# A fused scan and gated MLP: the opening's gate products by token tile, moments and copies handed between engines

## The chip, the core and the metric

The kernel runs on one core of one Trainium2 chip. Times are device microseconds of one execution. The kernel before took 182.35 us, the median of three runs (182.21 to 182.36). One further execution was profiled; its times are used for the working. The engines go by the profile's names: PE is TensorE's matmul, PEld its weight load, DVE is VectorE, ACT is ScalarE, POOL is GpSimd, and SP issues the DMAs (SPq is its queue).

## What is computed

There are 2048 tokens of width 448. A layer norm is followed by two branches that meet at the end:

```python
xn = layernorm(x)                                  # x: [1, 2048, 448]
# A: a diagonal complex recurrence over the tokens
Lam_bar = exp(exp(log_dt) * (Lambda_re + 1j * Lambda_im))
Bu = xn @ (((Lam_bar - 1) / Lam)[:, None] * B).T
h[t] = Lam_bar * h[t - 1] + Bu[t]
s = 2 * real(h @ C.T) + xn * Dskip
# B: a gated MLP, 448 -> 1792 -> 448
hF = sigmoid(xn @ w_gate) * (xn @ w_up)
out = x + s * silu(hF @ w_down)
```

Inputs and output are bfloat16.

## The kernel before

**Tiling.** The tokens go in four chunks of 512, each of four token tiles of 128. The MLP's 1792 features go in 14 feature tiles (`ft`) of 128. A product for one feature tile and one chunk has the features on the partitions and 512 tokens in one PSUM bank. The depth 448 is cut for the gate into three pieces of 128 rows and a tail of 64, and for the up product likewise with other pieces, so that the two tails (`wt`, rows 0 to 63 for the gate and 64 to 127 for up) run beside each other in the two halves of the array.

**Order.** Every engine runs its instructions in the order in which the program writes them (`keep_order`). A planner (`fill`, `rest`, `at`) lays VectorE's pieces of the recurrence between groups, and after the opening TensorE runs pairs of units (`group`, products of 64 rows at L514), the first of which is (4, 5), then (6, 7), (-1, 8), (-2, 9) and so on; negative numbers are the recurrence's input products `bu`. Eight PSUM banks are handed out in turn.

**The opening** is what lies ahead of group (4, 5). It is written out by hand, from L929 to L1015:

- SP's queue issues the token tiles of chunk 0, the weights' columns 0 to 511 (`load_w(sync, 0, 512)`, L150), columns 512 to 1279 with the tails first (L158), chunk 1's tokens, then, further down, four transposing loads of B (`emit_b`, L294), and columns 1280 to 1791 (L1025). ScalarE's queue issues the three vectors log_dt, Lambda_im and Lambda_re into `rows` (L142).
- TensorE runs products of no use (`warm`, L200) in stretches of 26, 5, 2 and 6, and between them turns the three vectors (`turn_twice`, L205 to L207, into `tp_v`) and the first two normed token tiles (`ln_turn`, L286, four transposes into `tp_x`).
- The layer norm of tiles 0, 1 and 3 takes its moments by VectorE (`ln_stats`, L216 and L217), its root by ScalarE as a Ln and an Exp (`ln_inv`, L249 and L250). Tile 2's moments are sums by ScalarE (L224, L227, L231) and its root is a power by POOL (L244). VectorE writes the normed tile (`ln_norm`, L272) and copies the turned tile out of PSUM (`ln_out`, L289) for all four tiles.
- ScalarE copies the turned vectors (`emit_vecs`, L316), makes dt (L321), from which POOL makes the angles (`emit_angles`, L326 to L328). ScalarE then makes the whole turns of four rows (`emit_whole`, L424), VectorE the fractions and their magnitudes (`emit_frac` L429, `emit_abs` L435), and ScalarE sines and cosines (L440, L443), after a table load that a dummy Silu brings (L962).
- Feature tiles 0 to 2 hold six banks. When tiles 0 and 1 are turned, the gate products of their 256 tokens run (L713), then the up products; the turns of tiles 2 and 3 lie between them. Then the tails' halves (L706) for 256 and 256 tokens, then feature tile 3, then the remaining products of tokens 256 to 511.
- ScalarE takes tanh of the gate (L719), VectorE halves the up product into `ub` (`up_copy`, L1000), and VectorE's product of the two (L723) gives `hF`. These free the banks for groups (4, 5) and (6, 7).

Of the kernel before, what the change touches and what calls it, by code (L numbers as in the profile page):

```python
# [14 lines left out]
ACT = mybir.ActivationFunctionType  # L15

S_TOK = 2048
D = 448
F = 1792
P = 128  # L20
TC = 512
HC = TC // 2
# [10 lines left out]
GATE_K, UP_K = (0, 2, 3), (0, 1, 3)  # L33
# [3 lines left out]
MAGIC = 12582912.0  # L37
CLAMP = 1.0 - 2e-6
LN_AND_EXP = 6
SIN_SCALE = TWO_PI * CLAMP  # L40


# [29 lines left out]
def kernel(  # L72
# [17 lines left out]
    nc = tc.nc  # L90
    pe, act, dve, pool, sync = nc.tensor, nc.scalar, nc.vector, nc.gpsimd, nc.sync
# [32 lines left out]
    def load_w(eng, f0, f1, tails_first=False):  # L124
        def rows(mat, r0, r1):
            m = mat[r0:r1, f0:f1]
            return m.rearrange("(kt p) f -> p kt f", p=P) if r1 - r0 > P else m

        eng.dma_start(out=wg[:, 1:3, f0:f1], in_=rows(B_w_gate, 192, 448))
        eng.dma_start(out=wg[:, 0, f0:f1], in_=rows(B_w_gate, 0, 128))  # L130
        up = ((wu[:, 0:2, f0:f1], rows(B_w_up, 0, 256)), (wu[:, 2, f0:f1], rows(B_w_up, 320, 448)))
        tails = ((wt[0:64, f0:f1], rows(B_w_gate, 128, 192)), (wt[64:128, f0:f1], rows(B_w_up, 256, 320)))
        for o, i in (tails + up if tails_first else up + tails):
            eng.dma_start(out=o, in_=i)
# [20 lines left out]
            x_t.append(w.tile([P, TPC, D], BF16, name="x3", tag="tc_re"))  # L155
        sync.dma_start(out=x_t[c][:], in_=x_src[:, c * TPC:(c + 1) * TPC, :])

    load_w(sync, 512, 1280, True)  # L158
    load_x(1)

    ctr = {}
# [36 lines left out]
    def warm(n, t=ident):  # L198
        for _ in range(n):
            pe.matmul(warm_ps[:], lhsT=t[:, 0:P], rhs=t[:, 0:P], start=True, stop=True)  # L200
# [13 lines left out]
    def ln_stats(t):  # L214
        stats = cp.tile([P, 6], FP32, name="stats")
        dve.bn_stats(out=stats[:], in_=x_t[t // TPC][:, t % TPC, :])  # L216
        dve.bn_aggr(out=mv[:, t, :], in_=stats[:])  # L217
# [4 lines left out]
    def ln_sum(t):  # L222
        c, j = divmod(t, TPC)
        act.activation(junk[:], x_t[c][:, j, :], ACT.Copy, accum_out=sums[:, t, 0:1])  # L224

    def ln_mean(t, n):
        act.activation(mv[:, t:t + n, 0:1], sums[:, t:t + n, 0:1], ACT.Copy, scale=1.0 / D)  # L227

    def ln_square(t):
        c, j = divmod(t, TPC)  # L230
        act.activation(junk[:], x_t[c][:, j, :], ACT.Square, bias=mv[:, t, 0:1], scale=-1.0,  # L231
                       accum_out=sums[:, t, 1:2])
# [15 lines left out]
    def ln_inv(t):  # L248
        act.activation(lnv[:, t, :], mv[:, t, 1:2], ACT.Ln, bias=epsb[:])  # L249
        act.activation(rsd[:, t, :], lnv[:, t, :], ACT.Exp, scale=-0.5)  # L250

    def ln_pow_of(t, n, var, scale):
        pool.tensor_scalar(out=ve[:, t:t + n, :], in0=var, scalar1=scale, scalar2=EPS, op0=ALU.mult, op1=ALU.add)
        ln_pow(t, n)
# [30 lines left out]
        for kt in range(KT):  # L285
            pe.transpose(tps[j % 2][:, kt, :], xb[:, j, K_ROWS[kt]:K_ROWS[kt] + P], ident[:])  # L286

    def ln_out(j):
        dve.tensor_copy(out=xnT[0][:, :, j * P:(j + 1) * P], in_=tps[j % 2][:])  # L289

# [21 lines left out]
    def emit_vecs():  # L314
        vec = w.tile([P, KT, 3], FP32, name="vec")
        act.copy(out=vec[:], in_=tp_v[:, :, 0:3])  # L316
        K.update(vec=vec)

    def emit_dt():
        vec, dt_b = K["vec"], w.tile([P, KT], BF16, name="dt_b")  # L320
        act.activation(dt_b[:], vec[:, :, 0], ACT.Exp)  # L321
        K.update(dt=dt_b, lim=vec[:, :, 1], lre=vec[:, :, 2])

    def emit_angles():
        theta, arg_r, turn, r_col = col("theta"), col("arg_r"), col("turn"), col("r_col")
        pool.tensor_tensor(out=theta[:], in0=K["dt"][:], in1=K["lim"], op=ALU.mult)  # L326
        pool.tensor_single_scalar(out=turn[:], in_=theta[:], scalar=1.0 / TWO_PI, op=ALU.mult)
        pool.tensor_tensor(out=arg_r[:], in0=K["dt"][:], in1=K["lre"], op=ALU.mult)  # L328
        K.update(arg=arg_r)
        K.update(theta=theta, turn=turn, r=r_col)  # L330
# [12 lines left out]
    def emit_anf():  # L343
        dve.tensor_single_scalar(out=K["anf"][:].bitcast(I32), in_=K["nf"][:].bitcast(I32), scalar=0x7FFFFFFF,
                                 op=ALU.bitwise_and)
# [76 lines left out]
    def emit_whole(pt):  # L422
        whole = sp.tile([P, HC], I32, name="whole", tag=("ta", "tb", "tcs", "tb")[pt])
        act.activation(whole[:], iota_f[:], ACT.Copy, scale=K["turn"][:, pt:pt + 1])  # L424
        K[pt] = whole

    def emit_frac(pt):
        f = sp.tile([P, HC], FP32, name="frac", tag="wv")
        dve.scalar_tensor_tensor(out=f[:], in0=iota_f[:], scalar=K["turn"][:, pt:pt + 1], in1=K[pt][:],  # L429
                                 op0=ALU.mult, op1=ALU.subtract)  # L430
        K[pt] = f

    def emit_abs(pt):
        af = sp.tile([P, HC], FP32, name="afrac", tag="td")
        dve.tensor_single_scalar(out=af[:].bitcast(I32), in_=K[pt][:].bitcast(I32), scalar=0x7FFFFFFF,  # L435
                                 op=ALU.bitwise_and)
        K[pt, 1] = af

    def emit_sin(pt):
        act.activation(spm[:, pt, 0, HC:TC], K[pt][:], ACT.Sin, scale=(SIN_SCALE if pt < 3 else sgp[:, 0:1]))  # L440

    def emit_cos(pt):
        act.activation(cosT[:, pt, HC:TC], K[pt, 1][:], ACT.Sin, scale=-TWO_PI, bias=hpi[:])  # L443
# [7 lines left out]
    def emit_neg(pt):  # L451
        dve.tensor_single_scalar(out=spm[:, pt, 1, HC:TC], in_=spm[:, pt, 0, HC:TC], scalar=-1.0, op=ALU.mult)
# [251 lines left out]
    def gu_half(c, ft, i, t, first, n0, n1):  # L704
        p0, kt = ((0, 1), (64, 2))[i]
        pe.matmul(t[:, n0:n1], lhsT=wt[p0:p0 + 64, ft * P:(ft + 1) * P], rhs=xnT[c][p0:p0 + 64, kt, n0:n1],  # L706
                  start=first, stop=not first)

    def gu_wholes(c, ft, gt, ut, first, n0=0, n1=TC, which=(0, 1), ks=(0, 1, 2), last=True):
        f0, f1 = ft * P, (ft + 1) * P  # L710
        for t, wm, kts in [((gt, wg, GATE_K), (ut, wu, UP_K))[i] for i in which]:
            for k in ks:
                pe.matmul(t[:, n0:n1], lhsT=wm[:, k, f0:f1], rhs=xnT[c][:, kts[k], n0:n1],  # L713
                          start=(first and k == 0), stop=(not first and last and k == 2))


    def gu_out(ft, gt, ub):
# [191 lines left out]
    def ln_plan(c):  # L909
# [14 lines left out]
        for j in range(TPC):  # L924
# [3 lines left out]
    dummy = w.tile([P, 1], FP32, name="dummy")  # L928
    act.add_instruction(mybir.InstLoadActFuncSet(name=nc.get_next_instruction_name(), act_func_set_id=LN_AND_EXP,  # L929
                                                 ins=[], outs=[]))  # L930
    warm(26, junk)
    turn_twice(tp_v, rows, 3)
    tps = [ps.tile([P, KT, P], BF16, name="tp_x", tag="bank", bufs=8) for _ in range(2)]
    gus = [(bank("g_ps"), bank("u_ps")) for _ in range(3)]
    warm(5)

    ln_stats(0)
    ln_inv(0)
    emit_vecs()
    ln_stats(1)  # L940
    ln_inv(1)
    emit_dt()
    emit_angles()
    ln_sum(2)
    ln_norm(0, 0)
    ln_turn(0, 0)
    warm(2)
    ln_norm(0, 1)
    ln_turn(0, 1)
    warm(6)  # L950
    ln_out(0)
    ln_out(1)
    ln_mean(2, 1)
    ln_square(2)
    ln_pow_of(2, 1, sums[:, 2:3, 1:2], 1.0 / D)
    ln_stats(3)
    emit_whole(0)
    ln_inv(3)
    for pt in (1, 3, 2):
        emit_whole(pt)  # L960
    act.activation(K["r"][:], K["arg"][:], ACT.Exp)
    act.activation(dummy[:], hpi[:], ACT.Silu)  # L962

    emit_frac(0)
    ln_norm(0, 2)
    ln_norm(0, 3)
    for ft in range(3):
        gu_wholes(0, ft, *gus[ft], True, 0, HC, (0,))
    for ft in range(3):
        gu_wholes(0, ft, *gus[ft], True, 0, HC, (1,), (0, 1))  # L970
    ln_turn(0, 2)
    ln_out(2)
    for ft in range(3):
        gu_wholes(0, ft, *gus[ft], False, 0, HC, (1,), (2,), False)
    ln_turn(0, 3)
    ln_out(3)
    emit_abs(0)
    for pt in (1, 3, 2):
        emit_frac(pt)
        emit_abs(pt)  # L980
    gus.append((bank("g_ps"), bank("u_ps")))
    for n0 in (0, HC):
        for ft in range(3):
            for i in range(2):
                gu_half(0, ft, i, gus[ft][i], n0 > 0, n0, n0 + HC)
    for i in range(2):
        gu_half(0, 3, i, gus[3][i], True, 0, TC)
    for ft in range(4):
        gu_wholes(0, ft, *gus[ft], False, (0 if ft == 3 else HC), TC)
    emit_steps()  # L990
    emit_den()
    for pt in (0, 1, 3):
        emit_sin(pt)
        emit_cos(pt)
        if pt == 0:
            emit_neg(pt)
    ubs = [fp.tile([P, TC], BF16, name="ub") for _ in range(4)]

    def up_copy(ft):
        dve.tensor_single_scalar(out=ubs[ft][:], in_=gus[ft][1][:], scalar=0.5, op=ALU.mult)  # L1000

    for ft in range(4):
        gu_out(ft, gus[ft][0], ubs[ft])
        up_copy(ft)
        if ft == 1:
            emit_neg(1)
            emit_neg(3)
            emit_sin(2)
            emit_cos(2)
            emit_anf()  # L1010
            emit_step_sines()
    emit_neg(2)
    for pt, ft in ((0, 5), (1, 5), (2, 8), (3, 11)):
        at(0, ft, 0.0, lambda pt=pt: emit_mirror(pt))
# [7 lines left out]
    for cc in range(2):  # L1022
        for kt in (0, 2):
            emit_b(cc, kt)
    load_w(sync, 1280, F)  # L1025
    sync.dma_start(out=skip[:], in_=A_Dskip.partition_broadcast(P))
    load_x(2)

# [140 lines left out]
```

## Time and profile before

| | |
|---|---|
| median of three runs | 182.35 us (182.21 to 182.36) |
| the profiled execution | 182.26 us |
| its span | 180.5 us (1.76 us lie around it) |
| PE busy | 176.2 us, 98% of the span |
| DVE busy | 163.4 us, 91% |
| ACT busy | 115.1 us, 64% |
| POOL busy | 23.1 us, 13% |
| first gate product starts | 6.38 us |
| group (4, 5) starts | 13.56 us |

A line of the timeline gives the start and the length in us, the engine, the source line, the operation, what it writes and reads, the shape and how many instructions are merged into the line; in brackets stands the idle time before it and who ended it. Products overlap in the array, so the length of a merged line holds a fixed tail of some 0.2 us after the last start; the starts tell the pace. A line of the waits names who waited, for whom, and then us in total, times and the longest. A DMA line ends with the time from issue to landing.

### The profile page before, as it was taken

What the parts mean: (1) busy time and instruction counts of PE and PEld (TensorE: products, weight loads), DVE (VectorE), ACT (ScalarE), POOL (GpSimd) and SP (SyncE); (2) the same over time, 40 slices, a digit from 0 to 9 for tenths busy, and PEclk for the clock granted to TensorE, in tenths of its full rate; (3) what the DMA queues carried; (4) which work ended last, traced back from release to release, by engine and by line L of the source; (5) the groups of instructions that cost most, each with busy time, mean ns of one, the idle gap of its engine ahead of it and who ended that gap; (6) DMA issues with size and microseconds to landing.
All of it is one profiled execution on the core that took longest, in us unless ns stands there. A gap on an engine that the chain in (4) does not pass through costs nothing.

```text
span 180.5 us, 4326 instructions
## 1 busy us (share of the span) xinstructions
PE 176.2 (98%) x1637; PEld 88.2 (49%) x1637; DVE 163.4 (91%) x332; ACT 115.1 (64%) x240; POOL 23.1 (13%) x54
## 2 busy tenths in 40 slices
PE   7999999999999999999999999999999999999992
PEld 7764444445544444544544444544554444545552
DVE  4889999899999879999999999599999999499993
ACT  4999878979577887988177667047137577144100
POOL 3525668522000000003000000000000000000000
PEclk9999999999999999999999999999999999999999
DMA  5899998983442005021710020030010100011012
GB/s 150 239 292 211 245 176 168 356 185 77 99 83 53 16 4 131 5 69 36 89 31 0 4 56 2 4 102 0 4 29 0 35 0 2 4 53 51 0 32 73
DMA packets 26348, 14.27 MB, mean 79 GB/s; under 512 B 16083, under 2 KB 26070, under 8 KB 26326
## 3 DMA queue, kind: packets, MB, share of 16 engines
q1 hardware_dynamic: 26320, 13.98, 33.7%
q8 instruction: 13, 0.21, 0.5%
q14 instruction: 9, 0.07, 0.2%
q10 hardware_dynamic: 6, 0.00, 0.0%
HBM read 7.69 MB, written 1.84 MB: 53 GB/s over the span
## 4 chain that ended last, share of the span: by engine, by line
PE 97%; DVE 1%; issue 0%; DVEq 0%
PE g_ps L514 25%; PE u_ps L514 19%; PE d_ps L514 18%; PE bu L514 12%; PE y_ps L514 11%; PE d_ps L1112 6%; PE warm_ps L200 2%; PE g_ps L713 2%; PE u_ps L713 1%; PE tp_x L286 1%; DVE sg L860 0%; PE g_ps L706 0%; DVE o_l L866 0%; PE u_ps L706 0%; DVE xnT L289 0%
## 5 line engine op out<-in xcount | busy, mean ns | idle before, releaser
L514 PE MATMUL u_ps<-xnT,wu 64*128 64x512 bf16 x312 | 61.4, 376 | 0.0
L514 PE MATMUL g_ps<-xnT,wg 64*128 64x512 bf16 x312 | 53.4, 376 | 0.0
L752 ACT ACTIVATE sig<-g_ps 128x512 bf16<-128x512 f32 x52 | 29.2, 597 | 28.6 <-PE g_ps L514 28.0
L514 PE MATMUL bu<-xnT,bT 64*128 64x512 bf16 x168 | 37.4, 376 | 0.0
L514 PE MATMUL d_ps<-wd,hF 64*128 64x448 bf16 x336 | 32.3, 349 | 0.0
L514 PEld LDWEIGHTS <-wu 64*128 64x128 bf16 x312 | 22.4, 94 | 18.5
L752 ACT CAST ub<-u_ps 128x512 bf16<-128x512 f32 x52 | 29.3, 606 | 0.9 <-DVE hF L723 0.8
L514 PEld LDWEIGHTS <-wg 64*128 64x128 bf16 x312 | 18.9, 94 | 18.3 <-issue 0.4
L514 PEld LDWEIGHTS <-hF 64*128 64x128 bf16 x336 | 16.4, 94 | 15.6
L611 DVE TENSOR_TENSOR_SCAN wv<-r_col,st,ta 128x512 bf16<-128x512 f32 x18 | 22.7, 1277 | 0.2
L514 PE MATMUL y_ps<-ct,h 64*128 64x448 bf16 (+2 forms) x203 | 22.1, 343 | 0.0
L749 DVE TENSOR_TENSOR hF<-sig,ub 128x512 bf16<-128x512 bf16 x52 | 21.0, 413 | 0.4 <-ACT ub L752 0.3
L514 PEld LDWEIGHTS <-bT 64*128 64x128 bf16 x168 | 15.8, 94 | 10.0
L514 PE MATMUL g_ps<-xnT,wt 64*128 64x512 bf16 x52 | 19.6, 376 | 0.0
L514 PE MATMUL u_ps<-xnT,wt 64*128 64x512 bf16 x52 | 19.6, 376 | 0.0
L514 PEld LDWEIGHTS <-h 64*128 64x128 bf16 (+1 forms) x203 | 11.6, 95 | 9.9
L776 ACT ACTIVATE sigd<-d_ps 128x448 bf16<-128x448 f32 x12 | 6.6, 553 | 15.0 <-PE d_ps L514 15.0
L592 ACT CAST bus<-bu 128x512 bf16<-128x512 f32 x24 | 14.3, 597 | 1.7 <-PE bu L514 1.6
L514 PEld LDWEIGHTS <-wt 64*128 64x128 bf16 x104 | 9.8, 94 | 6.2
L831 DVE TENSOR_TENSOR o_t<-y_ps,xn 128x448 bf16<-128x448 f32 x12 | 6.9, 617 | 4.8 <-PE y_ps L514 4.8
L1112 PE MATMUL d_ps<-wd,hF 128*128 128x448 bf16 x56 | 10.9, 353 | 0.0
L244 POOL TENSOR_TENSOR rsd<-ve,mhalf 128x2 f32<-128x2 f32 (+2 forms) x5 | 4.6, 922 | 44.2 <-PE bu L514 44.1
(153 smaller groups left out, 239.7 us busy)
## 6 DMA issues: line engine op xcount, KB each, us to landing
wd<-in_B_w_down_dram SPq DMA_DIRECT2D x1, 1568.0 KB, 7.3
x<-in_A_x_dram SPq DMA_DIRECT2D x3, 448.0 KB, 5.0
out_dram<-o_t SPq DMA_DIRECT2D x6, 224.0 KB, 2.1
wg<-in_B_w_gate_dram SPq DMA_DIRECT2D x2, 256.0 KB, 3.6
wu<-in_B_w_up_dram SPq DMA_DIRECT2D x2, 256.0 KB, 3.7
bsw<-bus SPq DMA_DIRECT2D x4, 128.0 KB, 2.8
wsw<-wv SPq DMA_DIRECT2D x8, 64.0 KB, 1.9
c_re<-in_A_C_re_dram SPq DMA_DIRECT2D x1, 392.0 KB
```

The costliest lines, as they stand in the source:

```text
L200: pe.matmul(warm_ps[:], lhsT=t[:, 0:P], rhs=t[:, 0:P], start=True, stop=True)
L244: pool.tensor_tensor(out=rsd[:, t:t + n, :], in0=ve[:, t:t + n, :], in1=mhalf[:, 0:n, :], op=ALU.pow)
L286: pe.transpose(tps[j % 2][:, kt, :], xb[:, j, K_ROWS[kt]:K_ROWS[kt] + P], ident[:])
L514: m = pe.matmul(self.t[:, n0:n1], lhsT=lhsT, rhs=rhs, start=self.done == 1, stop=self.done == self.n)
L592: empty = [lambda cc=cc: act.copy(out=bus[:, cc, :], in_=pst[cc][:]) for cc in range(2)]
L611: dve.tensor_tensor_scan(out=T["wv"][:, cc, :], data0=rb, data1=T["ta"][:, cc, :], initial=(0.0 if c == 0 else st[pt][:, cc, :]), op0=mul, ...
L713: pe.matmul(t[:, n0:n1], lhsT=wm[:, k, f0:f1], rhs=xnT[c][:, kts[k], n0:n1], start=(first and k == 0), stop=(not first and last and k == 2))
L749: dve.tensor_tensor(out=h[:], in0=sig[:], in1=ub[:], op=ALU.mult)
L752: u.empty = [lambda: act.activation(sig[:], gt[:], ACT.Sigmoid), lambda: act.copy(out=ub[:], in_=ut[:])]
L776: act.activation(sigd[:], ds[j][:], ACT.Sigmoid)
L831: dve.tensor_tensor(out=two_runs(o[:, i, :], HD, HD), in0=two_runs(ys[c, j + 2 * i][:], HD, HD), in1=xn_runs(c, j + 2 * i), op=ALU.add)
L1112: pe.matmul(ds[j][:], lhsT=hF[c, ft][:, j * P:(j + 1) * P], rhs=wd[:, ft, :], start=ft == 0, stop=ft == FT - 1)
```

## The change

Only the opening and the cut between two weight loads change. What it does, engine by engine:

- **TensorE**: 17 products ahead of the turn of the vectors in place of 26, 14 behind it in place of 5, and 3 in place of 6 after the turn of tile 1. The gate products of feature tiles 0 to 2 run for token tile 0 alone (128 columns) and then for token tile 1, depth piece by depth piece over the three feature tiles. Each bank is opened by one product with `start`; all later ones add with `start=False`, also to columns not yet written. The tails' halves of tokens 256 to 511 run by token tile as well.
- **ScalarE**: the vectors, dt and the angles come ahead of the roots of tiles 0 and 1; whole turns 0 and 1 come ahead of the norms. It copies turned tile 1 out of PSUM. It no longer takes tile 2's moments, and it makes tile 2's root. The table is loaded by an explicit instruction. Tanh of feature tiles 0 and 1 comes after the first sine and cosine, tanh 2 after the third pair, tanh 3 after the last.
- **VectorE**: moments of tiles 2 and 3 one after the other behind the copy of tile 0. Fractions 0 and 1 come behind the copy of tile 3, fractions 3 and 2 behind the first two up copies.
- **POOL**: tile 2's power goes.
- **SP**: the second weight load has columns 512 to 1151 and the last one columns 1152 to 1791.

```diff
-    load_w(sync, 512, 1280, True)
+    load_w(sync, 512, 1152, True)
...
-    def ln_out(j):
-        dve.tensor_copy(out=xnT[0][:, :, j * P:(j + 1) * P], in_=tps[j % 2][:])
+    def ln_out(j, by_act=False):
+        (act.copy if by_act else dve.tensor_copy)(out=xnT[0][:, :, j * P:(j + 1) * P], in_=tps[j % 2][:])
...
-                  start=first, stop=not first)
+                  start=first, stop=False)
...
+    def gu_whole(c, ft, i, t, k, n0, n1, first=False, last=False):
+        pe.matmul(t[:, n0:n1], lhsT=(wg, wu)[i][:, k, ft * P:(ft + 1) * P],
+                  rhs=xnT[c][:, (GATE_K, UP_K)[i][k], n0:n1], start=first, stop=last)
...
-    warm(26, junk)
+    warm(17, junk)
     turn_twice(tp_v, rows, 3)
...
-    warm(5)
-
+    warm(14)
+
+    emit_vecs()
+    emit_dt()
+    emit_angles()
     ln_stats(0)
     ln_inv(0)
-    emit_vecs()
     ln_stats(1)
     ln_inv(1)
-    emit_dt()
-    emit_angles()
-    ln_sum(2)
+    for pt in (0, 1):
+        emit_whole(pt)
     ln_norm(0, 0)
     ln_turn(0, 0)
     warm(2)
     ln_norm(0, 1)
     ln_turn(0, 1)
-    warm(6)
+    warm(3)
     ln_out(0)
-    ln_out(1)
-    ln_mean(2, 1)
-    ln_square(2)
-    ln_pow_of(2, 1, sums[:, 2:3, 1:2], 1.0 / D)
-    ln_stats(3)
-    emit_whole(0)
-    ln_inv(3)
-    for pt in (1, 3, 2):
-        emit_whole(pt)
+    ln_out(1, True)
+    emit_whole(3)
+    for t in (2, 3):
+        ln_stats(t)
+    for t in (2, 3):
+        ln_inv(t)
+    emit_whole(2)
     act.activation(K["r"][:], K["arg"][:], ACT.Exp)
-    act.activation(dummy[:], hpi[:], ACT.Silu)
-
-    emit_frac(0)
+    act.add_instruction(mybir.InstLoadActFuncSet(name=nc.get_next_instruction_name(), act_func_set_id=SILU_AND_SIN,
+                                                 ins=[], outs=[]))
     ln_norm(0, 2)
     ln_norm(0, 3)
-    for ft in range(3):
-        gu_wholes(0, ft, *gus[ft], True, 0, HC, (0,))
-    for ft in range(3):
-        gu_wholes(0, ft, *gus[ft], True, 0, HC, (1,), (0, 1))
+
+    def firsts(i, ks, n0, n1, first=None):
+        for k in ks:
+            for ft in range(3):
+                gu_whole(0, ft, i, gus[ft][i], k, n0, n1, k == first)
+
+    firsts(0, (1, 2, 0), 0, P, 1)
+    firsts(0, (1, 2, 0), P, HC)
+    firsts(1, (0, 1), 0, HC, 0)
     ln_turn(0, 2)
     ln_out(2)
-    for ft in range(3):
-        gu_wholes(0, ft, *gus[ft], False, 0, HC, (1,), (2,), False)
+    firsts(1, (2,), 0, HC)
     ln_turn(0, 3)
     ln_out(3)
-    emit_abs(0)
-    for pt in (1, 3, 2):
+    for pt in (0, 1):
         emit_frac(pt)
         emit_abs(pt)
...
-    for n0 in (0, HC):
+    for n0, n1 in ((0, HC), (HC, HC + P), (HC + P, TC)):
         for ft in range(3):
             for i in range(2):
-                gu_half(0, ft, i, gus[ft][i], n0 > 0, n0, n0 + HC)
+                gu_half(0, ft, i, gus[ft][i], False, n0, n1)
...
+    tables(0)
+    out(0)
+    out(1)
+    emit_neg(0)
+    for pt in (3, 2):
+        emit_frac(pt)
+        emit_abs(pt)
+    tables(1)
+    tables(3)
+    emit_neg(1)
+    out(2)
+    emit_neg(3)
+    tables(2)
+    out(3)
...
-    load_w(sync, 1280, F)
+    load_w(sync, 1152, F)
```

Here `tables(pt)` is the sine and cosine of a row, and `out(ft)` is the tanh and the up copy of a feature tile. Up and whole products of tokens 256 to 511, and of feature tile 3, keep their order.

More of the change, by code (lines that the diff above doesn't have):

```diff
@@ L39 @@
 LN_AND_EXP = 6
+SILU_AND_SIN = 18
 SIN_SCALE = TWO_PI * CLAMP
@@ L706, in gu_half @@
         pe.matmul(t[:, n0:n1], lhsT=wt[p0:p0 + 64, ft * P:(ft + 1) * P], rhs=xnT[c][p0:p0 + 64, kt, n0:n1],
-                  start=first, stop=not first)
[L709 to L714, printed above, removed]
+                  start=first, stop=False)
+    def gu_whole(c, ft, i, t, k, n0, n1, first=False, last=False):
+        pe.matmul(t[:, n0:n1], lhsT=(wg, wu)[i][:, k, ft * P:(ft + 1) * P],
+                  rhs=xnT[c][:, (GATE_K, UP_K)[i][k], n0:n1], start=first, stop=last)
     def gu_out(ft, gt, ub):
@@ L988 @@
     for ft in range(4):
-        gu_wholes(0, ft, *gus[ft], False, (0 if ft == 3 else HC), TC)
+        for i in range(2):
+            for k in range(3):
+                gu_whole(0, ft, i, gus[ft][i], k, (0 if ft == 3 else HC), TC, last=k == 2)
     emit_steps()
     emit_den()
[L992 to L996, printed above, removed]
     ubs = [fp.tile([P, TC], BF16, name="ub") for _ in range(4)]
@@ L1000, in up_copy, with tables, out @@
         dve.tensor_single_scalar(out=ubs[ft][:], in_=gus[ft][1][:], scalar=0.5, op=ALU.mult)
-    for ft in range(4):
+    def tables(pt):
+        emit_sin(pt)
+        emit_cos(pt)
+    def out(ft):
         gu_out(ft, gus[ft][0], ubs[ft])
         up_copy(ft)
[L1005 to L1011, printed above, removed]
+    tables(0)
[12 more added lines that the diff above has]
+    out(3)
+    emit_anf()
+    emit_step_sines()
     emit_neg(2)
```

## The prediction

> **What bounds the kernel now.** I read the chain of work that ended last first, then the waits of TensorE, then TensorE's timeline over the opening. The chain (part 4 of the page) and TensorE's waits up to 40 us, each as engine, line and releaser with total us, times and longest:
>
> ```profile
> PE 97%; DVE 1%; issue 0%; DVEq 0%
> ```
> ```profile
> PE warm_ps L200 <- DVE junk L177: 1.0, 1, 1.0
> PE g_ps L713 <- DVE xnT L289: 0.2, 1, 0.2
> ```
>
> TensorE is the bound, and after the first gate product it waits for no one that this view names. The stream behind the opening is closed, so a change that touches only the opening is worth what it moves the start of the first group of pairs, (4, 5), and nothing else. The timeline of TensorE (start, length, line, operation, count):
>
> ```profile
> 3.86 0.23 PE L205 MATMUL tp_v<-ident,rows 3*128 3x3 bf16 x3
> ...
> 4.19 0.71 PE L200 MATMUL warm_ps<-ident 128*128 128x128 bf16 x5
> 4.70 0.63 PE L286 MATMUL tp_x<-ident,xn 128*128 128x128 bf16 x4
> ...
> 6.38 1.14 PE L713 MATMUL g_ps<-xnT,wg 128*128 128x256 bf16 x9 [0.18 <-DVE xnT L289]
> 7.43 0.83 PE L713 MATMUL u_ps<-xnT,wu 128*128 128x256 bf16 x6
> 8.09 0.39 PE L286 MATMUL tp_x<-ident,xn 128*128 128x128 bf16 x4
> 8.32 0.49 PE L713 MATMUL u_ps<-xnT,wu 128*128 128x256 bf16 x3
> 8.64 0.39 PE L286 MATMUL tp_x<-ident,xn 128*128 128x128 bf16 x4
> 8.96 0.28 PE L706 MATMUL g_ps<-xnT,wt 64*128 64x256 bf16 x1
> 9.15 0.28 PE L706 MATMUL u_ps<-xnT,wt 64*128 64x256 bf16 x1
> ...
> 10.20 0.50 PE L713 MATMUL g_ps<-xnT,wg 128*128 128x256 bf16 x3
> ...
> 13.56 0.82 PE L514 MATMUL g_ps<-xnT,wg 64*128 64x512 bf16 x6
> ```
>
> Starts of equal products stand 0.109 us apart at 256 columns, 0.216 at 512, and 0.055 for a transpose of 128. The work from 6.38 to 13.56 is then 36 products of 256 columns (3.92), six of 512 (1.30), eight transposes (0.44), six half pairs of 256 (0.65) and one of 512 (0.22): 6.53 us of the 7.18. The other 0.65 is what can be won there, and two pieces of it belong to the weights' DMAs:
>
> ```profile
> 7.42 0.33 PEld L713 LDWEIGHTS <-wu 128*128 128x128 bf16 x4 [0.18 <-DMA wu<-in_B_w_up_dram]
> ```
> ```profile
> wt<-in_B_w_up_dram SPq DMA_DIRECT2D x2, 64.0 KB, 4.4
> ```
>
> The first up product waits until wu lands (7.38 by the trace's semaphore records). The up half's tail weights were issued at 4.73 and landed 4.4 later, 9.11; that is why the up product of L706 starts at 9.15 and not beside the gate's at 8.96. The rest is the wait for tile 3's copy (DVE copies of L289, 8.52 to 9.49; next half product 9.54) and two changes between 64 and 128 rows, about 0.1 each, which stay.
>
> **Start of the change: rows, roots, tiles 0 and 1.** The three rows have landed at 3.03 by the semaphore records, but their turn stands behind 26 matmuls until 3.86. With 17, at 0.107 each, the last streams until 2.76, so the turn starts at about 3.09 and takes the 0.40 it took (3.86 to 4.26): 3.49. ScalarE now does vec (0.17) and dt (0.19) ahead of the roots of tile 0: vec 3.52, dt 3.73, Ln 3.82 to 4.11, Exp 4.15 to 4.35, against 3.65 to 4.18 before: **0.17 later** for tile 0. Tile 1's roots wait for its moments at 4.34 as before and end at 4.91 in both. The first norm ends at 4.79 (4.62), the second at 5.34 in both. TensorE has 14 warm-ups from 3.42, done streaming at 4.89, so the turn of tile 0 starts at 4.89 (4.70) and ends 5.52, its copy by VectorE (0.425) at 5.99. Turn 1 starts 5.53 and ends about 5.93. ScalarE's copy: no row has ScalarE copying this tile; its nearest are the 512-column casts of L592 and L752 (0.60) and a 256-column copy (0.44). I take 0.58, the nearest by size; ends 0.44 and 0.68. Whole 0 and 1 run 4.9 to 5.71 (turn is ready at 4.63 by the POOL rows), so the copy runs 5.97 to 6.55.
>
> **Gates by tile.** Nine products of 128 columns from 6.03, nine more from 6.60. No product of 128 columns with 128 rows of weights is shown at this place; the transposes, of the same shape with a weight load each, stand 0.055 apart, and 0.109 (the row at 256) is the other end. By 0.055: 6.03 to 6.53 and 6.60 to 7.10. By 0.109 they would end at 7.6. So the gates end 0.26 sooner than the 7.36 of before, and then **wu is still not there until 7.38**. The up products start at 7.43 in both: the gain is given back.
>
> **Tiles 2 and 3.** VectorE drops the copy of tile 1 (0.43) and frac 0 (0.48) here and gains the moments of tile 2 (0.62+0.18, 0.75 pipelined). From the end of copy 0: moments until 6.73 and 7.46. ScalarE drops its moments (0.56, 0.20, 0.67 and two reads of 0.19) and POOL its power (0.19+0.58), and ScalarE has its copy, whole 3 (0.40), then roots of tile 2 until 7.38 and of tile 3 until 8.03 (Ln 0.29, Exp 0.20, 0.04 between). Norm 2 ends at 7.81; turn 2 needs it at 8.09. Norm 3 ends at 8.46 (8.27 before); turn 3 reads it at 8.54, TensorE's own order. Cover 0.08 to 0.28: no gain, no loss. Copies 2 and 3 then stand where they stood, 8.52 to 9.49.
>
> **Halves.** The first 256 columns still wait for 9.11. Then three pairs of 128 on tile 2 and three on tile 3 in place of three of 256: the pairs on tile 2 fill the time that was lost waiting for copy 3. By 0.055 a pair the 512 pair starts at 9.80 (9.87); by 0.109 it would be 10.1. I take 0.055: **gain 0.07**. For the row pairs the two ends give -0.07 and +0.26.
>
> **Tanh sooner, tables later.** Tanh 0 and 1 move from 12.55-13.61 to about 10.7-11.9, their up copies to 12.25. The first group reuses those banks at 13.56, so this only keeps the 0.07 from being stopped there. The fracs, sines and cosines of rows 1, 3 and 2 move behind it; ScalarE's last tanh still ends near 15.4 and the last up copy near 15.3, and group (6, 7) wants those banks at 16.5. Cover over 1 us; worth nothing.
>
> **Weight columns.** 128 columns (229 KB) move from the first late load to the second, which is queued on SP behind four transposes. They hold feature tile 9. The last load's final piece landed at 23.05 with 512 columns (semaphore records); 640 columns take 0.25 x (23.05 - 20.14) = 0.73 longer, 23.78, and pair (-2, 9) reads it at about 23.8. But 229 KB less stand ahead of the transposes, 0.8 us at the 292 GB/s of the page's slice from 9.0 to 13.5, so I put it at 23.0. Cost 0; without that cover 0 to 0.2.
>
> **Sum.** -0.07 us. The profiled execution took 182.26 us, span 180.5 and 1.76 around it; it becomes 180.43 and 182.19. The median of the runs is 0.09 above this execution, so the forecast is 182.28.
>
> **Rivals.**
> *Weights land sooner* (the two DMA waits shrink, by less traffic or by chance). With wu and wt in time the limits are norm 2 (7.81), norm 3 (8.46) and copy 3 at 9.40; then the 512 pair starts at 9.62: -0.25, 182.1. Against it: everything ahead of them in the queue is unchanged. Chance 0.13, half of it beyond 0.2%.
>
> *The clock comes late* (the slower side). Early transposes last 314 ns, the later ones 219, and the spacing of matmuls falls from 0.107 to 0.055 at 5.59, where the trace's clock record begins full grant; until there TensorE had been nearly unbroken since 0.97, 4.62 us. The change puts a hole of about 0.33 at 2.76 (0.13 before) and moves the small row turns right behind it. If such a hole counts as a break, full clock comes 4.62 after 3.09 to 3.42, at 7.7 to 8.0; the gates then run at 0.107 to about 7.9, the ups start 0.4 to 0.6 late, and 0.2 to 0.5 remains after the wait for wt: 182.55 to 182.85. It decides only if a hole between 0.13 and 0.33 matters, so chance 0.12. [...]
>
> *Tile 0's roots late.* vec and dt now stand ahead of them on ScalarE, with the row turn ahead of those. If the rows land d later than 3.03, everything up to turn 3 is d late; beyond 0.1 the cover at 8.54 is gone. A d of 0.5 gives +0.35, 182.7. Chance 0.08.
>
> *Small products at 0.109*: up to +0.26, 182.6; chance 0.08. *Feature tile 9's weights late*: +0.2, 182.55; chance 0.04.
>
> **How the numbers follow.** The forecast has 0.55, within 0.15 of 182.28. About 0.2% (0.36 us) is what a measurement of this kernel tells from no change. Faster than that: half of the first rival, 0.06. Slower: most of the clock (0.09), of the late roots (0.06), and parts of the last two (0.05), 0.20. Within: 0.74. The range is 182.0 to 183.0: below it is almost nothing, since even with all weights in time the copies leave 0.25; above it is the long end of the clock.
>
> **What would show it.** In the new profile: the row turn at 3.1; tile 0's gates near 6.0 and the last gate near 7.1; a gap of 0.3 before the first up product, released by wu at about 7.4; L706 still held until 9.1; group (4, 5) at 13.5. A spacing of 0.107 after 5.6 shows the clock rival. An up product before 7.2, or a first group before 13.3, would make the forecast wrong on the weights; a new wait of TensorE between 20 and 25 us would show the moved columns.

## The result, and the profile after

The changed kernel takes 182.83 us (median of 21 runs, 182.22 to 183.91); the kernel before, run beside it, 182.42 us (21 runs, 182.17 to 182.76). The ratio on record is 1.0028, with a 95% interval of 1.0014 to 1.0041 (the medians alone would give 1.0022). The change makes the kernel a little slower, and it spreads the times: 7 of its 21 executions lie above 183.0 us, none of the kernel before. (Beside the experiments below, 4 of 124 executions of the kernel before do.) The experiments found two losses of that size, late weights and a late clock. They were looked for in different places, because no single execution need show both.

The profiled execution of the changed kernel took 182.79 us, span 181.0, 0.5 more than the profiled execution of before. The line numbers of the changed kernel stand one to a few lines further on: 514 becomes 515, 713 becomes 711, 706 becomes 707. Busy time by engine, the chain of work that ended last, and TensorE's waits are now:

```profile
PE 176.3 (97%) x1648; PEld 93.5 (52%) x1649; DVE 165.1 (91%) x333; ACT 114.6 (63%) x237; POOL 23.1 (13%) x52
```
```profile
PE 94%; DMA 2%; SPq 1%; DVE 1%; issue 0%; POOLq 0%; DVEq 0%
```
```profile
PE warm_ps L201 <- DVE junk L178: 1.0, 1, 1.0
PE tp_v L206 <- DMA rows<-in_A_Lambda_re_dram: 0.3, 1, 0.3
```

TensorE has the same work (176.3 us against 176.2), yet the chain of the end has changed: 2% of it is now a DMA. Ahead of reading why, the opening by TensorE's timeline:

```profile
0.97 2.00 PE L201 MATMUL warm_ps<-junk 128*128 128x128 bf16 x17 [0.97 <-DVE junk L178]
3.31 0.21 PE L206 MATMUL tp_v<-ident,rows 3*128 3x3 bf16 x3 [0.34 <-DMA rows<-in_A_Lambda_re_dram]
...
3.62 1.68 PE L201 MATMUL warm_ps<-ident 128*128 128x128 bf16 x14
5.09 0.63 PE L287 MATMUL tp_x<-ident,xn 128*128 128x128 bf16 x4
...
6.24 1.26 PE L711 MATMUL g_ps<-xnT,wg 128*128 128x128 bf16 x18
7.58 0.83 PE L711 MATMUL u_ps<-xnT,wu 128*128 128x256 bf16 x6
...
9.12 0.28 PE L707 MATMUL g_ps<-xnT,wt 64*128 64x256 bf16 x1
...
9.87 0.38 PE L707 MATMUL g_ps<-xnT,wt 64*128 64x512 bf16 x1
...
13.56 0.61 PE L515 MATMUL g_ps<-xnT,wg 64*128 64x512 bf16 x4
```

Down the first column: the row turn begins 0.55 sooner than before (3.31, not 3.86), the gates 0.14 sooner (6.24), the up products 0.15 later (7.58), and group (4, 5) where it was (13.56). The opening has won nothing and lost nothing. The whole 0.5 comes in pair (-2, 9), where the trace has TensorE's weight loads wait:

```profile
23.45 0.09 PEld L515 LDWEIGHTS <-wu 64*128 64x128 bf16 x1 [0.28 <-DMA wu<-in_B_w_up_dram]
...
23.95 0.09 PEld L515 LDWEIGHTS <-wu 64*128 64x128 bf16 x1 [0.35 <-DMA wu<-in_B_w_up_dram]
...
24.44 0.09 PEld L515 LDWEIGHTS <-wt 64*128 64x128 bf16 x1 [0.40 <-DMA wt<-in_B_w_up_dram]
```

These are three pieces of feature tile 9's weights, the columns that moved to the last load. By the trace's semaphore records, wu's two pieces landed at 23.40 and 23.90 and the up tail's at 24.40, and each wait ends about 0.05 later. The pair took 3.545 us in place of 3.02: 0.52, all of the difference in span.

That is the middle of the changed kernel's times, but not their upper end: 183.9 needs another 1.1 us. The experiments had to find that too.

### The profile page after: what moved, and what is told of

Its sections match the earlier page's. It is cut to its first block, busy times and chain, and to the rows that moved or that the text cites. A ratio compares the mean times of both kernels' runs of the same rounds, so it can differ in the third digit from the quotient of the medians.

```text
span 181.0 us, 4343 instructions
## 1 busy us (share of the span) xinstructions
PE 176.3 (97%) x1648; PEld 93.5 (52%) x1649; DVE 165.1 (91%) x333; ACT 114.6 (63%) x237; POOL 23.1 (13%) x52
## 4 chain that ended last, share of the span: by engine, by line
PE 94%; DMA 2%; SPq 1%; DVE 1%; issue 0%; POOLq 0%; DVEq 0%
PE u_ps L515 24%; PE g_ps L515 20%; PE d_ps L515 17%; PE bu L515 12%; PE y_ps L515 11%; PE d_ps L1122 6%; DMA wu<-in_B_w_up_dram 2%; PE u_ps L711 2%; PE g_ps L711 1%; PE g_ps L707 1%; DVE sg L858 0%; DVE o_l L864 0%; SPq L131 0%; SPq L130 0%; PE tp_x L287 0%
## 5 line engine op out<-in xcount | busy, mean ns | idle before, releaser
L515 PE MATMUL g_ps<-xnT,wg 64*128 64x512 bf16 x312 | 60.6, 376 | 0.0
L515 PE MATMUL u_ps<-xnT,wu 64*128 64x512 bf16 x312 | 54.3, 376 | 0.0
L515 PE MATMUL bu<-xnT,bT 64*128 64x512 bf16 x168 | 36.1, 376 | 0.0
L515 PE MATMUL d_ps<-wd,hF 64*128 64x448 bf16 x336 | 32.9, 349 | 0.0
L515 PEld LDWEIGHTS <-wg 64*128 64x128 bf16 x312 | 22.0, 94 | 18.5 <-issue 0.4
L515 PEld LDWEIGHTS <-wu 64*128 64x128 bf16 x312 | 19.3, 94 | 18.8 <-DMA wu<-in_B_w_up_dram 0.6
L515 PEld LDWEIGHTS <-hF 64*128 64x128 bf16 x336 | 19.9, 94 | 12.1
L515 PEld LDWEIGHTS <-bT 64*128 64x128 bf16 x168 | 14.8, 94 | 10.2
L515 PEld LDWEIGHTS <-h 64*128 64x128 bf16 (+1 forms) x203 | 13.4, 95 | 8.0
L245 POOL TENSOR_TENSOR rsd<-ve,mhalf 128x2 f32<-128x2 f32 (+1 forms) x4 | 4.4, 1108 | 45.8 <-PE bu L515 45.3
```

The source lines that it names most:

```text
L245: pool.tensor_tensor(out=rsd[:, t:t + n, :], in0=ve[:, t:t + n, :], in1=mhalf[:, 0:n, :], op=ALU.pow)
L515: m = pe.matmul(self.t[:, n0:n1], lhsT=lhsT, rhs=rhs, start=self.done == 1, stop=self.done == self.n)
```

## The experiments

In the expectations, W is the theory that the moved weight columns cost the time. C, later C2, is the clock rival: the full clock comes late in some executions, because TensorE pauses at the sooner row turn; a clock "at its edge" is one that comes in time in some executions and late in others. O is the rival that something else in the rearranged opening is slower. "Full clock at" is where the trace's clock record goes to 1.00; it was 5.59 before and 5.82 after, in the profiled executions. Matmuls of 128 columns start 0.107 us apart until then and 0.055 from then on. As each kernel was run beside the kernel before, medians are given with that one's in brackets.

**1. The columns put back; 2. the columns alone; 3. a last load as short as before.** The first is the change with the old cut, the second the kernel before with the new cut. The third keeps the new cut, but loads feature tile 13's columns only later, ahead of `w_down`.

```diff
-    load_w(sync, 512, 1152, True)     # run 1, on the changed kernel; run 2 is the reverse, on the kernel before
+    load_w(sync, 512, 1280, True)
...
-    load_w(sync, 1152, F)
+    load_w(sync, 1280, F)
```
```diff
-    load_w(sync, 1152, F)             # run 3, on the changed kernel
+    load_w(sync, 1152, 1664)
...
+    at(0, 8, 0.0, lambda: load_w(sync, 1664, F))
     at(0, 8, 0.0, lambda: sync.dma_start(out=wd[:], in_=B_w_down.rearrange("(ft p) d -> p ft d", p=P)))
```

> The change, but with the second weight load back to columns 512 to 1279 and the last one from 1280. Theory W (the changed kernel is slower because feature tile 9's weights now come with the last load and land too late for pair (-2, 9); the opening itself gains nothing since it waits for wu): no wait of TensorE between 20 and 26 us, time 182.2 to 182.5 and runs as close together as those of before. Rival C (the hole ahead of the row turn makes the full clock come late in part of the runs): still 182.8 with single runs up to 183.9. Rival O (the rearranged opening is itself slower): 182.7 to 182.9, group (4, 5) later than 13.56.

> The kernel before with only the cut between the two weight loads moved from column 1280 to 1152. Theory W: 182.8 to 182.9, runs spread over a microsecond or more, weight loads of pair (-2, 9) wait for wu and wt near 23.5 to 24.4 us. Rivals C and O: as before, 182.4, since the opening is that of before.

> The change with its cut at 1152, but the last load brings columns 1152 to 1663 (rows of 1024 bytes) and feature tile 13's 128 columns follow ahead of w_down. Theory W: the load's last piece lands near 22 to 23.4 in place of 24.4, pair (-2, 9) waits at most 0.1, time 182.2 to 182.5. If rows of 1280 bytes are what made the load slow, it lands near 22; if the stretch is slow for any row, near 23.4. Rivals C and O: still 182.8.

Run 1 took 182.53 us [182.39], ratio 1.0017 (1.0002 to 1.0032): nine of its twelve executions are at most 182.84, three are at 183.10 to 183.76. So more than the columns is at work. The profiled execution was the longest, 183.76, and has no wait for weights in the pairs. What it shows is the clock, full only at 9.48:

```profile
3.34 0.21 PE L206 MATMUL tp_v<-ident,rows 3*128 3x3 bf16 x3 [0.37 <-DMA rows<-in_A_Lambda_re_dram]
...
3.65 1.68 PE L201 MATMUL warm_ps<-ident 128*128 128x128 bf16 x14
...
6.50 2.13 PE L711 MATMUL g_ps<-xnT,wg 128*128 128x128 bf16 x18
8.43 1.34 PE L711 MATMUL u_ps<-xnT,wu 128*128 128x256 bf16 x6
...
14.91 0.39 PE L515 MATMUL g_ps<-xnT,wg 64*128 64x512 bf16 x2
```

The eighteen gates take 2.13 us where the changed kernel's own trace has 1.26, and group (4, 5) starts at 14.91, 1.35 late. That is enough for the upper end.

Run 2 took 182.69 [182.39], ratio 1.0023 (1.0009 to 1.0038), from the cut alone. Its profiled execution (184.01, the longest) has the clock full at 3.75 and opens at 13.64, 0.08 behind the kernel before. Then it waits for the last piece of feature tile 9, which landed at 25.62:

```profile
25.67 0.09 PEld L514 LDWEIGHTS <-wt 64*128 64x128 bf16 x1 [1.68 <-DMA wt<-in_B_w_up_dram]
```

W is right as far as it goes: the columns cost time without any of the rest, though the median is below the 182.8 expected. And as the clock was in time here, late weights alone can reach the upper end too.

Run 3 took 183.85 (four executions), ratio 1.008 (1.0067 to 1.0093), and did not take the loss away. It waits at its own late columns (the second line), and still waits for tile 9's tail (the first), although the load that holds it is as short as before; its opening was 0.39 late besides. By the expectation, rows of 1280 bytes as the cause would have shown in a landing near 22, since this load has rows of 1024 bytes. It landed at 24.76.

```profile
24.80 0.09 PEld L515 LDWEIGHTS <-wt 64*128 64x128 bf16 x1 [0.61 <-DMA wt<-in_B_w_up_dram]
...
34.39 0.09 PEld L515 LDWEIGHTS <-wt 64*128 64x128 bf16 x1 [0.84 <-DMA wt<-in_B_w_up_dram]
```

**4. The pause made longer; 5 and 6. the pause filled.** All on the products ahead of the row turn: 6 or 21 of them on the kernel of run 1 (runs 4 and 5), 21 on the changed kernel (run 6).

```diff
-    warm(17, junk)
+    warm(6, junk)      # run 4; runs 5 and 6: warm(21, junk)
     turn_twice(tp_v, rows, 3)
```

> The first experiment's kernel with 6 matmuls of no use ahead of the row turn in place of 17, so that TensorE stands still from 1.6 to about 3.1 us. Rival C: a hole postpones the full clock from about 5.7 to 7.7 or later, gates at 0.107 us apart, time 0.3 us or more above the first experiment. Theory W expects the clock to matter only if the gates end after wu has landed at 7.4 to 7.6: full clock still at 5.6 to 5.9 and the first experiment's time within 0.15, or, if the clock does slip, a loss of 0.2 to 0.9.

> The first experiment's kernel (the change, cut back at column 1280) with 21 matmuls of no use ahead of the row turn in place of 17: they stream until about 3.2 us, when the rows have landed, so the hole is closed and nothing else moves. [...] Rival O (something else of the new opening makes the slow runs): still 182.5 with single runs of 183.1 to 183.8.

> The change as it is, cut at 1152, with the same 21 matmuls. Theory C2 with W (feature tile 9's weights come too late, by an amount that differs from run to run): 0.2 to 0.5 above the filled kernel with its cut at 1280, 182.5 to 182.9, waits for wu or wt between 22 and 26 us in the trace, (4, 5) by 13.6. If the cut costs nothing of itself: the same as that kernel.

Run 4 took 183.54 [182.39], ratio 1.0052 (1.0033 to 1.007), with the clock full at 9.43. Work of no use was left out, nothing waits for it, and the kernel is 1 us slower than run 1. That is what the clock rival says. The line of the waits gives the size of the pause:

```profile
PE tp_v L206 <- DMA rows<-in_A_Lambda_re_dram: 1.6, 1, 1.6
```

By the clock rival, filling the pause should have brought back the time of before; it did not. Run 5 took 182.84 [182.43], ratio 1.0022 (1.0007 to 1.0037), and five of its twelve executions are above 183.0; run 6 took 182.71, ratio 1.0022 (1.0005 to 1.0039). In run 6's profiled execution (184.34) the rows landed late, so that the pause was there again (a wait of 0.6 us behind the 21 products), and the clock was full only at 10.16. A fill of fixed length doesn't cover a DMA that lands when it lands. Run 5's profiled execution (182.50) is not one of its five slow ones, so what those had isn't shown.

Run 6's trace shows something else: group (4, 5) starts at 15.57, 2.01 late, and no weight load waits for tile 9, though its last piece landed at 24.37, as late as in the changed kernel. A late opening hides the late weights behind it, so the two losses don't add up.

**7. A second fill; 9. the same with the new cut; 12. the second fill alone.** Eight products of no use in place of three ahead of the gates, which makes TensorE start them later. Run 7 is run 5 with that, run 9 the changed kernel with both fills, run 12 is run 1 (17 products) with the second fill only. The second hole, in the text of run 12, is the one that this second fill is to close.

```diff
     ln_turn(0, 1)
-    warm(3)
+    warm(8)
     ln_out(0)
```

> The filled kernel (cut at 1280) with 8 matmuls of no use in place of 3 between the turn of tile 1 and the first gate product, 0.28 us more at full clock ahead of the gates. Theory W's other half (the earlier gates gain nothing since the up products wait for wu until 7.4 to 7.6): the first gates start 0.1 to 0.2 later, group (4, 5) no more than 0.1 later, time within 0.1 of the filled kernel. If the gates stand on the path: 0.2 or more slower.

> The change with its cut at 1152 and both stretches of useless matmuls lengthened (21 ahead of the row turn, 8 ahead of the gates), that is, the slack kernel with the cut of the change. Theory W: the cut costs what it cost alone on the kernel before, so 0.2 to 0.5 above the slack kernel's 182.44, 182.65 to 182.95, single runs up to 184. If the cut is free once the clock is steady: 182.4 to 182.5.

> The first experiment's kernel (cut at 1280, 17 ahead of the row turn) with 8 useless matmuls in place of 3 ahead of the gates. [...] If only the second hole matters: as the slack kernel, 182.44.

Run 7 took 182.44 [182.43], ratio 1.0003 (0.9993 to 1.0013), one execution of eleven above 183.0. The gates are off the path: five products more ahead of them cost nothing, since group (4, 5) started at 13.61, and the useless work brought the time back to that of before. Run 9 took 182.77 [182.45], ratio 1.0013 (0.9999 to 1.0027), with two above 183.0; against run 7, which differs by the cut, that fits W without showing it, since the intervals meet. Run 12 missed: 183.45 [182.45], ratio 1.0057 (1.0038 to 1.0076), all six executions above 183.0. With the pause left open (0.7 here, for the rows) the second fill saves nothing.

**8. The pause alone, on the kernel before.** This decides on the clock rival without any other part of the change. The number of useless products is cut from 26 to 17 ahead of the row turn and raised from 5 to 9 behind it.

```diff
-    warm(26, junk)
+    warm(17, junk)
     turn_twice(tp_v, rows, 3)
...
-    warm(5)
+    warm(9)
```

> The kernel before with only its matmuls of no use rearranged: 17 ahead of the row turn and 9 behind it (26 and 5), so that the hole is there and the first norms' turns start when they did. [...] Rival O: as before, 182.4, since all else is the kernel before.

It took 183.28 [182.43], ratio 1.0054 (1.0035 to 1.0072), with seven of nine executions above 183.0. The profiled one (184.54) had the clock full at 10.42, and group (4, 5) started at 15.83, 2.27 late:

```profile
4.04 0.22 PE L205 MATMUL tp_v<-ident,rows 3*128 3x3 bf16 x3 [1.07 <-DMA rows<-in_A_Lambda_re_dram]
...
7.13 2.08 PE L713 MATMUL g_ps<-xnT,wg 128*128 128x256 bf16 x9
9.01 1.48 PE L713 MATMUL u_ps<-xnT,wu 128*128 128x256 bf16 x6
...
14.65 0.59 PE L713 MATMUL g_ps<-xnT,wg 128*128 128x512 bf16 x2
```

The row turn was free to go sooner here as well. In this execution the rows landed so late that it went later (4.04, not 3.86), and everything behind it pays for the pause.

**10 and 11. What limits the opening once the clock is in time.** Run 10 is run 7 with another order of the first weight load: wu's first piece ahead of wg's last, and the gate's last piece multiplied behind the first up products. Run 11 adds the old order on ScalarE (roots ahead of vectors and dt, whole turns behind them) and ScalarE's copy of tile 1 ahead of the whole turns, with 10 products in place of 14 behind the row turn and 6 in place of 8 ahead of the gates.

```diff
+        up = up[:1] + g0 + up[1:] if up_early else up
...
-    firsts(0, (1, 2, 0), 0, P, 1)
-    firsts(0, (1, 2, 0), P, HC)
+    firsts(0, (1, 2), 0, P, 1)
+    firsts(0, (1, 2), P, HC)
     firsts(1, (0, 1), 0, HC, 0)
+    firsts(0, (0,), 0, HC)
```

> The slack kernel (cut at 1280, both fills) with the first weight load reordered, the up weights' first two pieces ahead of the gate's piece 0, and the gate's products of piece 0 behind the first up products. Theory W says the opening waits for wu; then the up products start near 7.0 in place of 7.5, the next limit is norm 3 and the copy of tile 3, and the time falls by 0.1 to 0.25 below the slack kernel, 182.2 to 182.35. If wu is no limit: 182.4 to 182.5.

> The kernel with the early up weights, and ScalarE's roots of tiles 0 and 1 ahead of vec and dt as in the kernel before, the copy of tile 1 ahead of the whole turns, 10 useless matmuls behind the row turn and 6 ahead of the gates. A late landing of the rows then no longer holds the norms, and tiles 2 and 3 come 0.2 to 0.3 sooner: 182.0 to 182.3 if the norms are the next limit; as the kernel with early up weights if the tails' weights (8.2 to 9.1) are; above 182.6 with single runs over 183 if 10 and 6 leave the clock at its edge again.

They took 182.38, ratio 0.9999 (0.9974 to 1.0023), and 182.60, ratio 1.0007 (0.999 to 1.0024) [182.45 for both]. Group (4, 5) started at 13.55 and 13.44, at most 0.12 sooner than before, and in both a new wait follows, for the second load's wu inside group (4, 5). Run 11's:

```profile
15.03 0.10 PEld L518 LDWEIGHTS <-wu 64*128 64x128 bf16 x2 [0.62 <-DMA wu<-in_B_w_up_dram]
```

In these two executions more was lost there than had been won ahead of it. Weights bound this part of the kernel from three sides, the first, the second and the last load.

**13 and 14. The sooner row turn undone.** Again 26 products, the row turn, and 5; ScalarE's roots ahead of the vectors and dt, and its whole turns behind its copy of tile 1; 6 products in place of 3 ahead of the gates. Gates by tile, the moments, the copy and the order of tanh stay as in the change. Run 13 has the old cut and run 14 the new one. **15 and 16. The pause put back into that, and a control.** Run 15 is run 14 with 17 and 9 products in place of 26 and 5; run 16 is run 14 again, beside it.

```diff
-    warm(17, junk)
+    warm(26, junk)     # runs 13, 14, 16; run 15 has 17 here and 9 below
     turn_twice(tp_v, rows, 3)
...
-    warm(14)
+    warm(5)
-    emit_vecs()
-    emit_dt()
-    emit_angles()
     ln_stats(0)
     ln_inv(0)
+    emit_vecs()
     ln_stats(1)
     ln_inv(1)
+    emit_dt()
+    emit_angles()
```

> The change with two things undone: the cut (back to 1280) and the sooner row turn (26 useless matmuls, row turn, 5; ScalarE's roots of tiles 0 and 1 ahead of vec and dt; 6 ahead of the gates; ScalarE's copy ahead of the whole turns). Gates by tile, VectorE's moments of all tiles, ScalarE's roots and copy and the tanh order stay. Theory C2: streaming from 1.0 to 3.7 is unbroken again, so the clock is full by 5.6 in most runs; 182.3 to 182.45, runs as close together as those of before, none over 182.9. If the scatter comes from elsewhere in the new opening: 182.5 or more with single runs over 183.1.

> The same with the cut of the change, 1152. Theory W: 0.15 to 0.5 above the kernel with the cut at 1280, single runs up to 184, weight loads of pair (-2, 9) waiting for wu or wt. If the cut is free: the same as the other.

> The kernel of the run with the sooner row turn undone and 1152 columns, in which only the 26 and 5 useless products around the row turn are made 17 and 9, so that the array pauses at about 2.8 us again. If the pause makes the clock late in a share of executions: a median of 182.7 or more, with single executions above 183.1 and others near 182.2. If the order on ScalarE (vectors and dt ahead of the roots) was what cost: as the control, about 182.4.

> The kernel with the sooner row turn undone and 1152 columns once more, unchanged, on the same chip as the one with the pause: 182.3 to 182.6, and level with the kernel before, if the first result was no luck of one chip.

Run 13 took 182.78 [182.60], ratio 1.0000 (0.9983 to 1.0017), and run 14 took 182.38 [182.60], ratio 0.9987 (0.9963 to 1.0010). Run 15 took 183.47 [182.47], ratio 1.0046 (1.0029 to 1.0063), five of six executions above 183.0; run 16 took 182.45 [182.47], ratio 1.0017 (0.9998 to 1.0037). Run 15's profiled execution has the clock full at 8.77:

```profile
3.45 0.21 PE L206 MATMUL tp_v<-ident,rows 3*128 3x3 bf16 x3 [0.48 <-DMA rows<-in_A_Lambda_re_dram]
...
6.87 2.08 PE L711 MATMUL g_ps<-xnT,wg 128*128 128x128 bf16 x18
...
14.75 0.61 PE L515 MATMUL g_ps<-xnT,wg 64*128 64x512 bf16 x4
```

and the control's has it at 4.71:

```profile
3.86 0.23 PE L206 MATMUL tp_v<-ident,rows 3*128 3x3 bf16 x3
...
5.99 1.17 PE L711 MATMUL g_ps<-xnT,wg 128*128 128x128 bf16 x18
...
13.34 0.82 PE L515 MATMUL g_ps<-xnT,wg 64*128 64x512 bf16 x6
```

On one chip, nine useless products fewer ahead of the row turn and four more behind it move the start of group (4, 5) by 1.41 us in the profiled executions and the median by 1.0. It is the pause, not ScalarE's order, since that is the same in both. And without the pause the rest of the change can't be told from the kernel before: no loss and no gain of it is shown. The control isn't clean, though: five of its twelve executions are at 183.1 to 183.7, and the other seven at 182.1 to 182.5; run 14, the same kernel, had one of twelve above 183.0. Which of the two losses those five had isn't known, as they were not profiled.

The control also shows W's other half. It starts group (4, 5) 0.22 sooner than the kernel before, its waits for feature tile 9's weights in pair (-2, 9) are 0.21, 0.17 and 0.33, and its span is 180.6 against 180.5. An opening that ends sooner reaches tile 9 sooner, but the last of these waits ends at 23.97, and run 14's last piece, with group (4, 5) 0.34 later (13.68), landed at 23.99: the weights did not come sooner by what the opening had won.

## Why the prediction was wrong

The forecast was no change, 182.28, with the range up to 183.0. The time came out slower by more than the measurement's doubt, at 182.83. The steps, one by one:

- **Row turn, 3.09: nearly.** It began at 3.31. The rows landed at 3.17 by the semaphore records, 0.14 later than in the trace of before, and the turn started 0.14 behind them, where the sum had 0.06. The first gate came at 6.24 for 6.03.
- **Gates at 0.055 and the gain given back: right.** Eighteen gates start in 1.04 us, the last at 7.28 (7.1 forecast), and then the up products wait for wu until about 7.5. They begin at 7.58 (7.43 forecast).
- **The halves held by wt till 9.11: right in time, wrong in cause.** They begin at 9.12, but wt had landed at 8.29 in this execution. TensorE's own order holds them now, the ups having started later.
- **Halves by tile, gain 0.07; group (4, 5) at 13.49: within 0.07.** The 512 pair starts at 9.87 (9.80 forecast, 9.87 before), and group (4, 5) at 13.56.
- **Tanh sooner worth nothing: right** as far as group (4, 5) goes, which waits for no bank.
- **Weight columns, "cost 0": this step failed.** It put the last piece of the last load at 23.0, by giving the load the time that 229 KB less ahead of the transposes would save. The transposes did come sooner: the fourth landed at 19.16, not 20.14, 0.98 against the 0.8 forecast. But the load's own part took longer than in proportion: 1147 KB in the 5.24 us behind that landing, where before it was 917 KB in 2.91 us. The last piece landed at 24.40. The prediction had 0.73 more for 25% more bytes; it is 2.33 more. The term that was mis-sized is the 2.91 itself. In the eleven traces whose last load has 917 KB, run 3 among them, it took 2.91 to 4.83, and the trace of before is the shortest by 0.70; in the seven with 1147 KB it took 3.53 to 5.37. The middle values are 4.33 and 4.23, so the extra bytes don't show in these traces. What the new cut changes is who reads first: tile 9's up tail is wanted at 23.94, where the first tile of the old last load, tile 10, wants its own at 26.96. The rows of this load, by issue, with KB each and the median time to landing, of after and then of before:

```profile
wg<-in_B_w_gate_dram SPq DMA_DIRECT2D x2, 320.0 KB, 4.5
wu<-in_B_w_up_dram SPq DMA_DIRECT2D x2, 320.0 KB, 5.0
```
```profile
wg<-in_B_w_gate_dram SPq DMA_DIRECT2D x2, 256.0 KB, 3.6
wu<-in_B_w_up_dram SPq DMA_DIRECT2D x2, 256.0 KB, 3.7
```

  (Each x2 joins two loads of equal size, the first load's among them before and the second's after.) The rival of that name had a chance of 0.04 and a price of 0.2; it cost 0.52 in the profiled execution, and the waits come to 1.9 in the worst one that was profiled (run 2). The error is one of method. Cover of 0.8 on a landing that had been seen once, and that was the earliest of its kind, was taken for certain.
- **The clock, 5.59: the second step that failed.** The prediction took the start of the full clock from one execution, as a property of the kernel, and asked only whether a hole of 0.33 would matter. It differs from execution to execution (3.62, 5.64 and 4.71 in runs 13, 14 and 16, which have one and the same order on TensorE), and the hole was larger than put: from 2.76, where the 17th product ends, to 3.62, if the row turn, five products of 3 columns, is not counted as work. The rival's price was low too (0.2 to 0.5; 1.35 in run 1's trace, 1.0 in the median of run 15 against its control). The range lays the long end of the clock above 183.0. The rival's own sum stops at 182.85, and no run of before shows a term that goes further; with the pause, runs 4, 8, 12 and 15 had medians of 183.28 to 183.54.

So the forecast's mechanism for the opening held, and both losses were named, but each as a thing that either happens or not. They would explain what the changed kernel does, which is a reading of one trace of it and of the variants: near 182.3 when both pass by (5 of 21 executions are at 182.22 to 182.50), some 0.5 more when tile 9's weights are late as in its trace, and about a microsecond more when the clock is late or the weights are as late as in run 2.

**What stays open.** How the 0.28% divides between the two: run 1 (the pause without the cut) gives 0.17% and run 2 (the cut without the pause) 0.23%, with intervals of 0.15% to each side, and only profiled executions tell which loss they had. The changed kernel itself was never profiled with a late clock. What makes the last load take 3 us in one execution and 5 in another isn't known either; longer rows are not needed for it, as run 3 shows. And why the new cut costs on the kernel before but not in run 14: run 14's last piece landed at 23.99, just ahead of its reading at 24.05, and the sooner second load may pay as well (in run 13, with the old cut, group (4, 5) waits 0.62 and 0.41 for the second load's wu, and in run 14 it does not), but that is an argument from one trace each. No version was shown to be faster than the kernel before; runs 7, 9, 10, 11, 13, 14 and 16 can't be told from it.

## What to carry to other kernels

A landing or a clock start read from one trace is a draw from a spread (here the three vectors had landed at 3.03 to 3.90 us, and the clock was full at 3.62 to 10.42); before a cover of a few tenths is priced at nothing, ask what happens when the DMA lands half a microsecond later. The useless matmuls that keep the array streaming ahead of the first real ones were part of this kernel: taking some out, so that the vectors' turn fell into a gap among them, had a price of 0.54% in run 8. And this opening, bound by weights landing, gave back what was won ahead of them: 0.12 us sooner at group (4, 5) in run 11, then 0.62 of waiting at the second load's wu.

## What the runs showed of the hardware

**The full clock starts at a different time from execution to execution, and past 7 us in seven of the eight traces with a wait for the rows.** In eighteen traces, all of openings that begin streaming at 0.97, the full clock began anywhere between 3.6 and 10.4 us, and in runs 13, 14 and 16, whose TensorE runs the same opening, at 3.62, 5.64 and 4.71. In the five traces with 26 products ahead of the row turn (before and runs 2, 13, 14 and 16), where TensorE does not wait for the rows, it began by 5.64. Where TensorE waited for them, it began at 5.82 (after, a wait of 0.34 us), 9.48 (run 1, 0.37), 8.77 (run 15, 0.48), 10.16 (run 6, 0.59), 10.42 (run 8, 1.07) and 9.43 (run 4, 1.58). For runs 3 (0.34) and 12 (0.69) the pace of the eighteen gates, which took 1.67 and 1.42 us, gives about 7.5 and 7.9, an estimate. The length of the wait doesn't put these in order, the same 0.34 goes with 5.82 and with 7.5, and how much of a pause makes the clock late isn't shown. The kernel before has no such wait in its trace; why three of its executions beside the experiments took 184.0 to 184.4 isn't known.

**The same DMA lands at different times.** Three vectors of 0.9 KB each, issued at the same place, had landed by 3.03 us before, 3.17 after, 3.85 in run 6 and 3.90 in run 8, by the semaphore records. Feature tile 9's last piece, under the same cut, landed at 23.2 (run 15), 24.0 (run 14), 24.4 (after) and 25.6 (run 2).
